# Gate/up loads moved onto the queue of the stores and fills, and a w_down half loaded sooner

## The chip, the cores and the metric

The kernel is one program on one NeuronCore of a Trainium2 chip. The metric is the device time of one launch in microseconds; lower is better. The kernel before took 619.9 us as the median of 8 runs (615.25 to 622.07 us). The profile is of one further execution, which took 621.76 us and whose span, from the core's first instruction to its last, is 620.0 us.

## The reference

The reference is the forward and the backward pass of a transformer block for one token (B = 1, S = 1, D = 1024), returned together. The parts that matter here, cut down:

```python
mod = silu(c) @ w_mod                      # six sections of 1024: sa, ca, ga, sb, cb, gb
h = layernorm(x) * (1 + ca) + sa
x = x + ga * attention(h)                  # 32 query heads, 4 kv heads, window of 4096 keys, Dh = 128
h = layernorm(x) * (1 + cb) + sb
g, u = h @ w_gate, h @ w_up                # 1024 x 3584 each
x = x + gb * ((sigmoid(g) * u) @ w_down)   # w_down is 3584 x 1024
# vjp with grad_out: gradients of x, k_cache, v_cache, wq, wo, w_gate, w_up, w_down, c, w_mod
```

All inputs and outputs are bf16. The gradients are large: those of `w_gate` and `w_up` are 7.3 MB each, that of `w_down` as much, and those of the two caches are 67 MB each. Only the last 4096 of 65,536 rows of a cache head take part, so most of the cache gradients is zero, and these zeros must be written too.

## The kernel before

The order of work is written out by hand, and each engine runs its own list in that order. All large buffers lie in one tile `arena`, whose places are reused again and again; whoever writes a place waits until its earlier readers and writers are done. Three queues issue transfers:

- SP's queue (hardware descriptors) issues most loads.
- POOL's queue (software descriptors) issues all large stores, a few loads, and the fills: `zero(n)` stores n megabytes (1 MiB each) of zeros into the cache gradients. There are 120 such pieces, and tables named `Z_...` say how many go where. Fills depend on nothing, so they keep the transfer engines supplied while the stores wait for compute.
- ACT's queue issues three tiny loads at the start.

Each queue issues in order. A transfer on POOL's queue also waits for the landing of the transfer issued eight places before it on that queue (eight semaphores go round), so at most eight POOL transfers are under way.

The parts in order: load the modulation weights, the keys, `wq` and the values; attention forward; two long matmul chains that make N (`n_ps`, L630) and B (`b_ps`, L683); the modulation sections; then the feed-forward stage, which is what the change touches; then the final stage, which computes and stores the other gradients.

Before the feed-forward stage, six tiles `B_t` (2 KiB per partition each) hold the product B. They are "parked": `park(p, ...)` transposes tile p into a PSUM bank, after which its place in the arena is free. Tiles 0 to 3 are parked early. Tiles 4 and 5 lie where the second half of a `w_down` block will lie, and are parked after the folds: `fold_tile` (L869) adds three modulation tiles on TensorE into two PSUM banks, which ScalarE copies out. The PSUM banks for this come from a rotation `rot`, at that point one bank of pool `psum` and two of pool `ppq`.

The feed-forward stage goes over 7 blocks q of 512 hidden columns. For each block:

- `load_ug` brings the block's columns of `w_up` and `w_gate` (2 MiB in all, rows of 1 KB) into one of two buffers; blocks q and q+2 share a buffer. `load_wd` brings the block's 512 rows of `w_down` in two halves of 512 KiB into one buffer.
- `front(q)` multiplies the loaded columns by h2 on TensorE, `gates` and `hh_ops` make the hidden values.
- For each half, `ffn_mm` uses `w_down` for the forward pass, `wd_ttr` (VectorE, L210, writing `junk`) for the backward pass, and `wd_outer` (VectorE, L206) overwrites the half by its gradient, which `store_wd` (L853, POOL) stores.
- `dug_part` makes the gradient of the gate/up activations as the row `dug_b`.
- In the loop over j, `ttr` (VectorE, L210) reads each of 8 slices of the gate/up buffer, `outer_act` (ScalarE, L241) overwrites it by its gradient, and `store_ug` (L867, POOL) stores slices 0-3, 4-5 and 6-7.

In the kernel before, `load_ug(q + 2, ...)` stands directly behind the store of the same slices and is issued by SP (L863), as is `load_wd` (L850). SP therefore waits, in turn, for the landing of each store and then issues the load into its place. Fills stand at three points of each iteration, `Z_FFN` gives the counts: after the store of slices 0-3, after the store of slices 6-7, and after the second `store_wd`. ScalarE also does `side()` jobs, transposes that later stages need, between these steps.

Of the kernel before, what the change touches and what calls it, by code (L numbers as in the profile page):

```python
# [10 lines left out]
P = 128  # L11
FP32 = mybir.dt.float32
BF16 = mybir.dt.bfloat16
# [6 lines left out]
D = 1024  # L20
# [27 lines left out]
Z_GA = 3  # L48
Z_CB = 2
Z_Q = [0] * 7 + [3]  # L50
# [4 lines left out]
Z_FOLD = (3, 4)  # L55
Z_FFN = [(1, 2, 2)] + [(1, 1, 2)] * 5 + [(2, 2, 2)]
Z_END = (3, 1, 1, 1, 1)

@with_exitstack
def kernel(  # L60
# [34 lines left out]
    px = ctx.enter_context(tc.tile_pool(name="px", bufs=1, space=bass.MemoryType.PSUM))  # L95
    ppq = ctx.enter_context(tc.tile_pool(name="ppq", bufs=2, space=bass.MemoryType.PSUM))

# [229 lines left out]
    B_off = [156, 158, 152, 154, 156, 158]  # L327
    B_t = [ar(o, 2) for o in B_off]

# [71 lines left out]

    rot[:] = [(psum, "mm"), (pna, "na"), (pgu, "gu"), (ppq, "pq"), (px, "x"), (pna, "na"), (ppq, "pq")]
    mod_ps = new_acc("mod_ps")
# [32 lines left out]

    jobs = []

    def side(n=1):
# [179 lines left out]
    for g in range(G):  # L619
        nbank = [(pna, ppq)[g % 2].tile([P, 512], FP32, name="n_ps", tag=("na", "pq")[g % 2]) for _ in range(2)]  # L620
        for t_ in range(KT):
# [50 lines left out]
    def bch(n=1):  # L672
        for _ in range(n):
            if not bq:
                return
            p, i, u = bq.pop(0)
            if i == 0:
                bbank[p] = [(pna, ppq)[p % 2].tile([P, 512], FP32, name="b_ps", tag=("na", "pq")[p % 2])
                            for _ in range(2)]
            for a in range(4):  # L680
                h = 4 * u + a
                for k in range(2):
                    mm = nc.tensor.matmul(bbank[p][k][:, :], lhsT=a4[:, p, h, :], rhs=wo_t[u][:, a, k * 512:(k + 1) * 512],  # L683
                                          start=(i == 0 and a == 0), stop=(i == 7 and a == 3))
            zero(Z_B[nbq - 1 - len(bq)], recent(mm, 3))
            if i == 7:
                for k in range(2):
                    o = B_t[p][:, k * 512:(k + 1) * 512]
                    if k == 0 or p == NBP - 1:
                        nc.scalar.copy(out=o, in_=bbank[p][k][:, :])  # L690
                    else:
                        cp(o, bbank[p][k][:, :])
# [132 lines left out]
    zero(Z_CB)  # L825
    rot[:] = [(psum, "mm"), (ppq, "pq"), (ppq, "pq")]

# [8 lines left out]
    jobs[:] = [tr_unit(v_nat[:, i // 4, (i % 4) * 1024:(i % 4 + 1) * 1024]) for i in range(16)]  # L836
    side(4)

# [21 lines left out]

    def load_ug(q, j0, n, eng=nc.sync):
        for k, view in ((0, wu_view), (1, wg_view)):
            eng.dma_start(out=ug_tile(q, k, j0, n), in_=ug_part(view, q, j0, n))  # L863

# [4 lines left out]
    def fold_tile(t):  # L869
# [11 lines left out]
        fold_ps.clear()  # L881

    fold_ps = []
    md_ps = new_acc("md_ps")
    for t in range(4):
        fold_tile(t)
    mod_tiles(md_ps, sb_t, range(4), True)
    load_ug(0, 0, 4, nc.gpsimd)
    load_ug(0, 4, 4, nc.gpsimd)
    load_wd(0, 0)  # L890
    zero(Z_FOLD[0])
# [8 lines left out]
    for t in range(4, 8):  # L900
        fold_tile(t)
    park(4, ppq, "pq")
    park(5, ppq, "pq")
    rot[:] = [(psum, "mm")]
    load_wd(0, 1)
    load_ug(1, 0, 4, nc.gpsimd)
    load_ug(1, 4, 4, nc.gpsimd)
    zero(Z_FOLD[1])
# [3 lines left out]
    dug_b2 = dug_b.rearrange("p (k f) -> p k f", k=2)  # L912
    junk = vt([P, D], "junk", BF16)
    dh2acc = vt([P, NB * KD], "dh2acc")
# [69 lines left out]
    for q in range(NB):  # L984
        z = Z_FFN[q]
        more = q + 1 < NB
        for j in range(KD):
            w = ug_v[:, q % 2, j // 4, j % 4, :, :].rearrange("p k f -> p (k f)")
            ttr(w, w, dug_b, dh2acc[:, q * KD + j:q * KD + j + 1])
            if j in (0, 2, 5) or (j == 6 and q < 4):  # L990
                side()
            outer_act(w, h2[:, j:j + 1], dug_b)
            if j == 0:
                if q == 0:
                    cp(ffn, ffn_ps)
# [39 lines left out]
    for p in range(NBP):  # L1035
        nc.scalar.copy(out=B_t[p], in_=BT_ps[p][:, :])
    rot[:] = [(psum, "mm"), (pna, "na"), (pgu, "gu"), (ppq, "pq"), (px, "x"), (pna, "na"), (ppq, "pq")]
    dh2 = vt([P, KD], "dh2")
# [269 lines left out]
```

## Time and profile before

| what | value |
|---|---|
| median of 8 runs | 619.9 us (615.25 to 622.07) |
| profiled execution, its time / its span | 621.76 us / 620.0 us |
| moved over HBM | 61.87 MB read, 185.60 MB written, 399 GB/s over the span |
| busy: PE, DVE, ACT, POOL | 391.9, 324.3, 282.1, 153.8 us |
| first stores of gate/up gradients, blocks 0 to 6, issued at | 319.06, 342.00, 376.50, 398.41, 420.87, 456.33, 477.16 us |

How to read it: an engine's busy time is no bound by itself. The page's row GB/s gives what the 16 transfer engines moved in each of 40 slices of 15.5 us. A long run of slices above 420 is a stretch in which transfers set the pace, and a slice well below it means that the transfer engines had nothing queued for part of it, or small pieces. The chain that ended last leads from the last instruction back to what released each step. A wait is listed as who waited, for whom, us in total, times, and the longest. The trace also has the time at which each transfer landed.

### The profile page before, as it was taken

What the parts mean: (1) busy time and instruction counts of PE and PEld (TensorE: products, weight loads), DVE (VectorE), ACT (ScalarE), POOL (GpSimd) and SP (SyncE); (2) the same over time, 40 slices, a digit from 0 to 9 for tenths busy, and PEclk for the clock granted to TensorE, in tenths of its full rate; (3) what the DMA queues carried; (4) which work ended last, traced back from release to release, by engine and by line L of the source; (5) the groups of instructions that cost most, each with busy time, mean ns of one, the idle gap of its engine ahead of it and who ended that gap; (6) DMA issues with size and microseconds to landing.
All of it is one profiled execution on the core that took longest, in us unless ns stands there. A gap on an engine that the chain in (4) does not pass through costs nothing.

```text
span 620.0 us, 10941 instructions
## 1 busy us (share of the span) xinstructions
PE 391.9 (63%) x4516; PEld 267.3 (43%) x4516; DVE 324.3 (52%) x616; ACT 282.1 (45%) x426; POOL 153.8 (25%) x249
## 2 busy tenths in 40 slices
PE   3996889999999989898244245341453466826200
PEld 3994434334345546558243234341342255826200
DVE  2745488999411020150468167772478279596500
ACT  3488414557211024246085438764287735834100
POOL 0002121222231212213223314323134442132220
PEclk9999598999999989998655555555555576555555
DMA  9999999999999999999999999999999999999995
GB/s 356 420 418 385 411 421 396 425 422 421 418 426 425 425 428 415 350 422 340 397 357 405 410 384 390 411 410 408 357 406 350 422 418 415 422 424 425 427 424 227
DMA packets 57105, 248.19 MB, mean 400 GB/s; under 512 B 5517, under 2 KB 15757, under 8 KB 36624
## 3 DMA queue, kind: packets, MB, share of 16 engines
q0 software_dynamic: 34656, 200.29, 84.1%
q1 hardware_dynamic: 22352, 47.20, 22.0%
q8 instruction: 35, 0.57, 0.4%
q14 instruction: 14, 0.11, 0.0%
q10 hardware_dynamic: 48, 0.01, 0.0%
HBM read 61.87 MB, written 185.60 MB: 399 GB/s over the span
## 4 chain that ended last, share of the span: by engine, by line
PE 39%; DMA 28%; DVE 12%; ACT 10%; issue 7%; POOL 1%; ACTq 0%; POOLq 0%; SPq 0%; DVEq 0%
PE b_ps L683 14%; DMA out_dram<-arena 14%; DMA arena<-in_B_w_down_dram 10%; PE n_ps L630 6%; ACT arena L241 4%; DVE junk L210 3%; DVE arena L193 3%; DMA out_dram<-zeros 3%; PE t_ps L592 2%; PE fold_ps L876 2%; ACT arena L833 2%; PE tp_wq L448 2%; DVE arena L210 1%; PE w_ps L393 1%; PE tp_side L832 1%
## 5 line engine op out<-in xcount | busy, mean ns | idle before, releaser
L169 POOL DMA_DIRECT2D out_dram<-zeros x114 | 62.9, 554 | 201.7 <-PE n_ps L630 54.9
L683 PE MATMUL b_ps<-arena 128*128 128x512 bf16 x384 | 89.7, 390 | 0.0
L832 PE MATMUL tp_side<-ident_bf,arena 128*128 128x128 bf16 x416 | 49.8, 297 | 53.4 <-ACT arena L833 44.8
L193 DVE TENSOR_TENSOR arena<-arena 128x2048 bf16<-128x2048 bf16 x64 | 76.6, 1223 | 3.4 <-PE n_ps L630 1.5
L630 PE MATMUL n_ps<-arena 128*128 128x512 bf16 x256 | 67.1, 386 | 6.1 <-DVE arena L193 4.5
L210 DVE CUSTOM_DVE_ANT_0 arena<-arena,scr 128x1024 bf16<-128x1024 bf16 x56 | 65.2, 1221 | 9.5 <-ACT scr L965 9.5
L833 ACT COPY arena<-tp_side 128x1024 bf16<-128x1024 bf16 x52 | 52.1, 1010 | 35.0 <-PE tp_side L832 34.8
L832 PEld LDWEIGHTS <-arena 128*128 128x128 bf16 x416 | 41.4, 137 | 58.9 <-issue 58.6
L241 ACT ACTIVATE arena<-scr,h 128x1024 bf16<-128x1024 bf16 x56 | 61.0, 1145 | 0.0
L683 PEld LDWEIGHTS <-arena 128*128 128x128 bf16 x384 | 37.7, 100 | 46.5 <-issue 7.3
L867 POOL DMA_DIRECT2D out_dram<-arena x42 | 30.8, 736 | 60.7 <-ACT arena L241 56.5
L630 PEld LDWEIGHTS <-arena 128*128 128x128 bf16 x256 | 25.1, 99 | 42.5 <-issue 18.0
L210 DVE CUSTOM_DVE_ANT_0 junk<-arena,b1k 128x1024 bf16<-128x1024 bf16 x28 | 34.2, 1223 | 13.7 <-DMA arena<-in_B_w_down_dram 13.2
L1129 ACT ACTIVATE arena<-ps_kv 128x512 bf16<-128x512 f32 x48 | 26.0, 687 | 32.3 <-PE ps_kv L1125 32.2
L1125 PE MATMUL ps_kv<-junk,arena 8*128 8x128 bf16 x256 | 27.2, 305 | 14.1 <-DVE arena L206 13.1
L594 ACT CAST arena<-t_ps 128x512 bf16<-128x512 f32 x56 | 30.1, 589 | 12.2 <-PE t_ps L592 12.2
L1125 PEld LDWEIGHTS <-arena 8*128 8x128 bf16 x256 | 25.3, 141 | 15.7 <-issue 15.7
L928 PE MATMUL fg<-h_bf,arena 128*128 128x1 bf16 x448 | 14.2, 166 | 25.9 <-DMA arena<-in_B_w_up_dram 18.9
L202 DVE CAST arena<-b_ps 128x512 bf16<-128x512 f32 x5 | 3.5, 692 | 47.1 <-PE b_ps L683 47.1
L853 POOL DMA_DIRECT2D out_dram<-arena x14 | 10.0, 717 | 63.9 <-DVE arena L206 57.2
L450 ACT COPY arena<-tp_wq 128x1024 bf16<-128x1024 bf16 x23 | 21.7, 1041 | 8.3 <-PE tp_wq L448 8.3
L928 PEld LDWEIGHTS <-arena 128*128 128x128 bf16 x448 | 13.6, 104 | 26.8 <-DMA arena<-in_B_w_up_dram 19.5
(294 smaller groups left out, 618.5 us busy)
## 6 DMA issues: line engine op xcount, KB each, us to landing
out_dram<-zeros POOLq DMA_DIRECT2D x114, 1024.0 KB, 11.3
out_dram<-arena POOLq DMA_DIRECT2D x32, 1024.0 KB, 19.4
out_dram<-arena POOLq DMA_DIRECT2D x36, 512.0 KB, 8.8
arena<-in_A_wq_dram SPq DMA_DIRECT2D x8, 1024.0 KB, 20.3
arena<-in_B_w_down_dram SPq DMA_DIRECT2D x14, 512.0 KB, 10.4
out_dram<-arena POOLq DMA_DIRECT2D x28, 256.0 KB, 8.4
arena<-in_A_wo_dram SPq DMA_DIRECT2D x6, 1024.0 KB, 6.7
arena<-in_w_mod_dram POOLq DMA_DIRECT2D x6, 1024.0 KB, 9.4
```

The source lines that it names most:

```text
L169: ins = nc.gpsimd.dma_start(out=region.bitcast(FP32), in_=zeros[:, :])
L193: return nc.vector.tensor_tensor(out=out, in0=a, in1=b, op=op)
L210: return nc.vector.tensor_tensor_reduce(out=out, in0=w, in1=b, scale=1.0, scalar=0.0, op0=ALU.mult, op1=ALU.add, accum_out=acc)
L241: return nc.scalar.activation(out=out, in_=b, func=ACT.Copy, scale=col)
L594: nc.scalar.copy(out=o, in_=ps)
L630: mm = nc.tensor.matmul(nbank[k][:, :], lhsT=k_nat[:, g, t_ * DH:(t_ + 1) * DH], rhs=vp[:, t_ % 2, 4 * k:4 * k + 4, :].rearrange("p h d -> ...
L683: mm = nc.tensor.matmul(bbank[p][k][:, :], lhsT=a4[:, p, h, :], rhs=wo_t[u][:, a, k * 512:(k + 1) * 512], start=(i == 0 and a == 0), stop= ...
L832: nc.tensor.transpose(tp[:, i * P:(i + 1) * P], blk[:, i * P:(i + 1) * P], ident_bf[:, :])
L833: nc.scalar.copy(out=blk, in_=tp[:, :])
L867: nc.gpsimd.dma_start(out=ug_part(view, q, j0, n), in_=ug_tile(q, k, j0, n))
L928: nc.tensor.matmul(gu[:, col + i:col + i + 1], lhsT=ug_v[:, q % 2, j // 4, j % 4, k, i * P:(i + 1) * P], rhs=h2_bf[:, j:j + 1], start=(j = ...
L1125: nc.tensor.matmul(ps[:, t4 * DH:(t4 + 1) * DH], lhsT=rows[32 * g:32 * g + HG, t_ * P:(t_ + 1) * P], rhs=hd[32 * g:32 * g + HG, :], start= ...
```

## The change

1. **Gate/up loads.** `load_ug` is issued by POOL for every block. In the loop it no longer stands behind the stores in the j loop. The load of slices 0-3 of block q+2 comes after the first `wd_ttr` of block q+1, that of slices 4-5 after the first `store_wd` and a fill, that of slices 6-7 after the second `store_wd`, ahead of a fill. SP's queue keeps only `w_down` loads in this stage.
2. **Fills.** `Z_FFN` has four points per iteration, one fill at each (31 fills before, 29 after, one fewer in the first block and one fewer in the last); `Z_CB`, ahead of the folds, goes from 2 to 3. One fill more is left over for the very end, where what is left is issued.
3. **B tiles.** Tile 5 lies in `junk` rather than in the arena; tile 4 is parked after the first of four `side` jobs, ahead of the folds. Both halves of `load_wd(0, ...)` then stand ahead of the folds.
4. **PSUM.** Pool `ppq` (two banks) becomes `ppq` and `prq` (one each), since tile 4 now occupies one of them from early on. The rotation for the folds has two banks rather than three.

```diff
-Z_CB = 2
+Z_CB = 3
-Z_FFN = [(1, 2, 2)] + [(1, 1, 2)] * 5 + [(2, 2, 2)]
+Z_FFN = [(1, 1, 1, 1)] * 6 + [(1, 2, 1, 1)]
...
-    ppq = ctx.enter_context(tc.tile_pool(name="ppq", bufs=2, space=bass.MemoryType.PSUM))
+    ppq = ctx.enter_context(tc.tile_pool(name="ppq", bufs=1, space=bass.MemoryType.PSUM))
+    prq = ctx.enter_context(tc.tile_pool(name="prq", bufs=1, space=bass.MemoryType.PSUM))
...
-    B_t = [ar(o, 2) for o in B_off]
+    junk = vt([P, D], "junk", BF16)
+    B_t = [ar(o, 2) for o in B_off[:5]] + [junk]
...
+    def bank_pair(name, odd):
+        pair = ((ppq, "pq"), (prq, "rq")) if odd % 2 else ((pna, "na"), (pna, "na"))
+        return [pl.tile([P, 512], FP32, name=name, tag=tag) for pl, tag in pair]
...
-    rot[:] = [(psum, "mm"), (ppq, "pq"), (ppq, "pq")]
+    rot[:] = [(psum, "mm"), (prq, "rq")]
...
-    side(4)
+    side(1)
+    park(4, ppq, "pq")
+    side(3)
...
-    def load_ug(q, j0, n, eng=nc.sync):
+    def load_ug(q, j0, n):
         for k, view in ((0, wu_view), (1, wg_view)):
-            eng.dma_start(out=ug_tile(q, k, j0, n), in_=ug_part(view, q, j0, n))
+            nc.gpsimd.dma_start(out=ug_tile(q, k, j0, n), in_=ug_part(view, q, j0, n))
...
+    load_wd(0, 0)
+    load_wd(0, 1)
     fold_ps = []
...
-    load_wd(0, 0)
     zero(Z_FOLD[0])
...
-    park(4, ppq, "pq")
-    park(5, ppq, "pq")
+    park(5, prq, "rq")
     rot[:] = [(psum, "mm")]
-    load_wd(0, 1)
...
             if j == 3:
                 store_ug(q, 0, 4)
                 zero(z[0])
-                if q + 2 < NB:
-                    load_ug(q + 2, 0, 4)
             if j == 5:
                 store_ug(q, 4, 2)
-                if q + 2 < NB:
-                    load_ug(q + 2, 4, 2)
         store_ug(q, 6, 2)
         zero(z[1])
         if more:
-            if q + 2 < NB:
-                load_ug(q + 2, 6, 2)
             front(q + 1)
             gates(q + 1)
             side()
             hh_ops(q + 1)
             ffn_mm(q + 1, 0)
             wd_ttr(q + 1, 0)
+            if q + 2 < NB:
+                load_ug(q + 2, 0, 4)
             wd_outer(q + 1, 0)
+            zero(z[2])
+            if q + 2 < NB:
+                load_ug(q + 2, 4, 2)
             side()
             ffn_mm(q + 1, 1)
             wd_ttr(q + 1, 1)
             side()
             dug_part(q + 1)
             wd_outer(q + 1, 1)
-            zero(z[2])
+            if q + 2 < NB:
+                load_ug(q + 2, 6, 2)
+            zero(z[3])
             if q + 2 < NB:
                 load_wd(q + 2, 0)
                 load_wd(q + 2, 1)
         else:
-            zero(z[2])
+            zero(z[2] + z[3])
```

The two places that allocated PSUM pairs for `n_ps` and `b_ps` call `bank_pair`, which gives the same banks under the new pool names.

More of the change, by code (lines that the diff above doesn't have):

```diff
@@ L400, in w01_fold @@
                 cp(o, v)
-    rot[:] = [(psum, "mm"), (pna, "na"), (pgu, "gu"), (ppq, "pq"), (px, "x"), (pna, "na"), (ppq, "pq")]
+    rot[:] = [(psum, "mm"), (pna, "na"), (pgu, "gu"), (ppq, "pq"), (px, "x"), (pna, "na"), (prq, "rq")]
     mod_ps = new_acc("mod_ps")
@@ L619 @@
     for g in range(G):
-        nbank = [(pna, ppq)[g % 2].tile([P, 512], FP32, name="n_ps", tag=("na", "pq")[g % 2]) for _ in range(2)]
+        nbank = bank_pair("n_ps", g)
         for t_ in range(KT):
@@ L677, in bch @@
             if i == 0:
-                bbank[p] = [(pna, ppq)[p % 2].tile([P, 512], FP32, name="b_ps", tag=("na", "pq")[p % 2])
-                            for _ in range(2)]
+                bbank[p] = bank_pair("b_ps", p)
             for a in range(4):
@@ L887 @@
     mod_tiles(md_ps, sb_t, range(4), True)
-    load_ug(0, 0, 4, nc.gpsimd)
-    load_ug(0, 4, 4, nc.gpsimd)
-    load_wd(0, 0)
+    load_ug(0, 0, 4)
+    load_ug(0, 4, 4)
     zero(Z_FOLD[0])
@@ L901 @@
         fold_tile(t)
-    park(4, ppq, "pq")
-    park(5, ppq, "pq")
+    park(5, prq, "rq")
     rot[:] = [(psum, "mm")]
-    load_wd(0, 1)
-    load_ug(1, 0, 4, nc.gpsimd)
-    load_ug(1, 4, 4, nc.gpsimd)
+    load_ug(1, 0, 4)
+    load_ug(1, 4, 4)
     zero(Z_FOLD[1])
@@ L912 @@
     dug_b2 = dug_b.rearrange("p (k f) -> p k f", k=2)
-    junk = vt([P, D], "junk", BF16)
     dh2acc = vt([P, NB * KD], "dh2acc")
@@ L1036 @@
         nc.scalar.copy(out=B_t[p], in_=BT_ps[p][:, :])
-    rot[:] = [(psum, "mm"), (pna, "na"), (pgu, "gu"), (ppq, "pq"), (px, "x"), (pna, "na"), (ppq, "pq")]
+    rot[:] = [(psum, "mm"), (pna, "na"), (pgu, "gu"), (ppq, "pq"), (px, "x"), (pna, "na"), (prq, "rq")]
     dh2 = vt([P, KD], "dh2")
```

## Prediction

> **What bounds the kernel now.** I read the page's throughput row first, then the waits, the chain, and last the windows and the issue times of one queue.
>
> ```profile
> GB/s 356 420 418 385 411 421 396 425 422 421 418 426 425 425 428 415 350 422 340 397 357 405 410 384 390 411 410 408 357 406 350 422 418 415 422 424 425 427 424 227
> ...
> q0 software_dynamic: 34656, 200.29, 84.1%
> q1 hardware_dynamic: 22352, 47.20, 22.0%
> ```
>
> Each number is 15.5 us. Most of the run moves 415 to 428 GB/s: the transfer engines set the pace. The weak part is slices 17 to 31 (248 to 480 us), the folds and the feed-forward stage. The sum below is therefore one of transfer time: the bytes stay the same, so time is won only where engines stood empty or moved slowly, and lost where new holes open. That part is 84% POOL's queue (q0) and else SP's (q1).
>
> ```profile
> SPq L863 <- DMA out_dram<-arena: 67.6, 24, 9.0
> ...
> SPq L850 <- DMA out_dram<-arena: 60.4, 12, 23.6
> ...
> POOL out_dram L853 <- DVE arena L206: 57.2, 11, 16.4
> POOL out_dram L867 <- ACT arena L241: 56.5, 17, 7.5
> ```
>
> SP waits for each store to land before a load may take its place, and POOL waits for compute (a `w_down` gradient from VectorE, a gate/up gradient from ScalarE). In POOL's waits the engines live on what is queued.
>
> ```profile
> 294.83 11.83 DMA arena<-in_B_w_down_dram
> ...
> 343.72 20.39 DMA arena<-in_B_w_down_dram
> ...
> 418.74 21.99 DMA arena<-in_B_w_down_dram
> ```
>
> In the chain (start, us, what), `w_down` loads take 20 and 22 us where the clean ones take 7.3 to 10.4 by their landings: SP issued them right behind six gate/up loads.
>
> ```profile
> 319.06 1.50 POOL L867 DMA_DIRECT2D out_dram<-arena  x2 [7.51 <-ACT arena L241]
> ...
> 342.00 1.52 POOL L867 DMA_DIRECT2D out_dram<-arena  x2 [6.68 <-ACT arena L241]
> ...
> 376.50 1.52 POOL L867 DMA_DIRECT2D out_dram<-arena  x2 [6.70 <-ACT arena L241]
> ...
> 456.33 1.52 POOL L867 DMA_DIRECT2D out_dram<-arena  x2 [6.67 <-ACT arena L241]
> ...
> 477.16 1.52 POOL L867 DMA_DIRECT2D out_dram<-arena  x2 [5.92 <-ACT arena L241]
> ```
>
> These are first stores of blocks 0, 1, 2, 5 and 6. The last step, 20.8 us, is compute alone: no loads are left. Blocks 0 to 5 take 137.3 us, 27.45 each, with steps of 34.5 and 35.5 where `front` or `wd_ttr` waited for a late load. A block moves 10.49 MB (gate/up 2.10 in and out, `w_down` 1.05 in and out, four fills 4.19), which is 24.7 us at 425 GB/s. So compute has room, and transfers and late loads share the blame.
>
> ```profile
> 284.00:286.00 2.00, 0.24 (x10) 0.24 (x10) 0.00 (x0) 0.71 (x1) 2.00 (x3) 1.00 0.63 162
> 302.00:304.00 2.00, 0.00 (x0) 0.00 (x0) 0.00 (x0) 0.00 (x0) 0.72 (x1) 0.50 1.04 362
> 318.00:320.00 2.00, 0.00 (x0) 0.00 (x0) 2.00 (x5) 2.00 (x3) 0.94 (x2) 0.50 0.43 169
> 448.00:450.00 2.00, 1.01 (x8) 0.85 (x8) 1.11 (x1) 0.90 (x2) 1.66 (x3) 0.50 0.56 209
> 464.00:466.00 2.00, 1.01 (x8) 0.74 (x7) 2.00 (x6) 0.90 (x2) 0.71 (x1) 0.50 1.05 410
> ```
>
> The last two columns are the engines' busy share and GB/s. At 284, 318 and 448 us the engines run dry (share 0.4 to 0.6). At 302 us they are busy at 362 GB/s, with POOL's gate/up loads in rows of 1 KB. At 464 us POOL's stores and fills alone give 410.
>
> **The change, step by step.** Durations are of the profiled execution: 621.76 us, 1.76 outside its 620.0 us span. Its median sibling is 619.9; I take the difference from the ledger and apply it to the median.
>
> **(a) Fold region.** Window 280:290 moves 305 GB/s, a hole of (425-305)*10/425 = 2.8 us. The added fill is 1.05 MB = 2.5 us, issued near 274.5 behind two others. The second `w_down` half, 0.52 MB = 1.2 us, was issued at 294.83 after tile 5's parking; now it needs only tile 4's, near 275. Together 3.7 us of supply for a hole of 2.8: -2.8. The first half was already issued at 253.11, so moving its line does nothing. Against it: the fill stands ahead of block 0's gate/up loads, which landed until 293.35, and `front(0)` began at 295.87, a slack of 2.5 us. So the bound is 0 to -2.8; I take -2.8, since the hole itself takes up the fill.
>
> **(b) Block 0.** VectorE waited for the late half until 306.69. Its work before ends near 302.4 (300.68 and two L206 of 0.88), so the second half starts 4.3 us earlier, the first store at 314.8 rather than 319.06. The fills ahead of it landed until 317.7; the hole in 318 to 322 (169 and 226 GB/s against 410, two us each: 1.2 + 0.9) closes: -2.1, bound 0 to -2.1. It does not shorten block 1 as much: its `w_down` loads wait for the first store's landing at 318.91, behind the same fills.
>
> **(c) Loads in one line.** In 320 to 449 us, 129 us at 395 GB/s, 51.0 MB go through. What is the rate in one line? By rows: block 1's four loads and one `w_down` half took 300.75 (landing of the fill ahead) to 307.9: 2.62 MB in 7.15 us, 367 GB/s. Gate/up loads 2.10/0.367 = 5.7 us, stores and fills 7.34/0.410 = 17.9, `w_down` loads 1.05/0.410 = 2.6: 26.2 us a block, 400 GB/s. Where the two queues ran together without holes (330 to 360 us) the windows show 404 to 413, say 407. I take the middle, 403: 51.0/0.403 = 126.5, -2.5 us. Ends: 400 gives -1.6, and 420 gives -7.7.
>
> A rule of the Trainium skill speaks against a gain in rate here: "DMA: Bandwidth & Descriptors", section "Issuing engines are not separate DMA queues", says that all issuers' transfers run on the same 16 engines and interleave, so the issuer saves only issue time. Reading the windows 190 to 230 us (POOL alone, 425) as what one line gives would make (c) -9.1 (51.0/0.425 = 119.9). But those are fills and no 1 KB loads; the 367 row is POOL's own. So I side with the rule: what (c) can win is the holes (366, 371, 382 and 321 GB/s in the 10-us windows from 320, 360, 380 and 440), not the mixing.
>
> **Waits that come with it.** POOL now issues 30 loads more in the loop, at 0.77 us (POOL's gate/up loads) 23 us, on 40 busy in 129: no bound. A load waits for the landing of the store it overwrites; that store stands eight places before it on the queue or near it, so the queue's own limit would have held it anyway. Behind a waiting load stand a `w_down` gradient store, for which SP's next load waits, and a fill. Relative to a block's first store t, and with the unstalled block (456.33, 465.18, 468.65): the `w_down` store is ready at t+8.9; the load before it is released when the first store pair, issued over 1.5 us, has landed. With landing time L, the load's own issue taking 1.5 us, the store goes at t+3+L, lands at t+3+2L, and SP's load lands Lw later; the next block's `wd_ttr` wants it at t+T+5.3. So T >= 2L + Lw - 2.3. With L = 8.6 and Lw = 8.7 (near the middle of the L867 and clean L850 landings) that is 23.6: under 26.2. The gate/up loads in last place follow the second `w_down` store, t+12.3, are out by t+13.8 and land by t+13.8+L, wanted at t+T+5: T >= 17.4.
>
> The second rule that speaks against: "SBUF — State Buffer", section "SBUF: two separate sides", says that VectorE in a two-port mode locks POOL out, so that POOL's queue cannot write descriptors while SP's is immune. By it, each of six loads a block could lose one L206 of 0.88 us, 5.3 us a block, 26 in five. The row: L867, the same shape, issued beside a VectorE that is busy over half of the time, has a mean of 736 ns against 770 for loads issued beside an idle one. I take the row: 0. If the rule held, the 9 us of queued transfers (L) would cover most of it.
>
> **(d) Small ones.** Two PSUM banks for the folds: TensorE takes about 0.87 us per bank (6.96 us for eight), ScalarE's copy 0.59, so the bank is free again while the other fills: 0, at most 0.2 us for eight tiles, 1.6. Parking tile 4 moves 0.61 us of TensorE. The fills taken from blocks 0 and 6 are in the bytes of (a) and of the end, where slices run at 422 to 427: 2.5 us of work moved, neither won nor lost. In blocks 5 and 6 nothing is left to load in either kernel, and the hole at 476 us (window 470:480, 323 GB/s) stays. For new small holes I charge +0.8, two rows like that at 446 us (306 against 410: 0.5 us each) less what the fill before the second half covers.
>
> Sum: -2.8 - 2.1 - 2.5 + 0.8 = -6.6 us; 621.76 would be 615.2, and the median 619.9 becomes **613.3 us**.
>
> **Rivals.**
> 1. Slower, by the loop above: the load that waits for its store holds back the `w_down` store. With L = 11 and Lw = 10, T is 29.7; for five blocks 5*(29.7-27.45) = +11.3, less (a) and (b) where they remain (half of 4.9), and the fill: about +6, 626 us. It decides from T near 28.5, that is L above 10.6 at Lw = 9.6. For it: landings of L867 stores of 10 to 13 us at 342 to 349 us, and 24 waits of SP for just these landings, which now are POOL's. Against it: L falls when fewer transfers are queued, and after the waiting load a block has 5 MB queued, over 12 us.
> 2. Hidden anyway: the fill only stands ahead of the loads of block 0, the earlier `w_down` half only lets VectorE wait for the next one, and the rate in line is 398 (-1). With half of (b) that is about 618 us. For it: block 1's loads wait for the store that lands at 318.91.
> 3. More: in-line loads overlap with stores, 420 GB/s: -7.7 in place of -2.5, 608 us. For it: 425 of POOL alone; against it: 362 and 367 with loads.
>
> **Numbers.** A measurement of this kernel tells about 0.5% (3.1 us) from no change. Likeliest 0.42 (613.3, its own range 610 to 616), rival 1 0.20, rival 2 0.22, rival 3 0.16. Faster (under 616.8): the likeliest, rival 3 and a tenth of rival 2, 0.60; same 0.20; slower (over 623.0) 0.20. The range 606 to 625 leaves out the better part of rival 3's gain below and half of rival 1 above.
>
> **What would show it.** (a) Window 280:290 above 380 GB/s and SP's second `w_down` issue near 275. (b) First store near 315, no row under 300 at 318 to 322. (c) First stores 25 to 27 us apart with no step above 30, no wait of TensorE L928 for a gate/up load over 3 us, `w_down` landings under 12 us, 400 to 408 GB/s in the stage. (d) Fold matmuls in no more than 7.2 us. It is wrong if POOL's waits for store landings at the load line pass 4 us a block and VectorE still waits for `w_down` (rival 1), or if first stores come no sooner (rival 2).

## The result and the profile after

| | before | after |
|---|---|---|
| median, us | 619.02 (614.6 to 626.48, 32 runs) | 612.41 (611.86 to 614.42, 11 runs) |
| ratio, 95% interval | 1 | 0.9905 (0.9878 to 0.9933) |
| profiled execution / its span, us | 621.76 / 620.0 | 612.05 / 610.3 |

The change makes the kernel faster by 6.6 us by the medians and by 5.9 us by the ratio; the interval reaches from 4.1 to 7.6. The ratios leave out slow runs of before, those more than 1.5% above its fastest, one of 957 us timed beside e1 to e4 among them. The profiled pair differs by 9.7 us, 3.1 more than the medians; below it turns out that 1.1 to 2.2 us of this difference arose ahead of everything the loads and fills touch.

The lines of after have other numbers than those of before:

| what | before | after |
|---|---|---|
| gate/up stores (POOL) | L867 | L874 |
| `w_down` stores (POOL) | L853 | L860 |
| gate/up loads | L863 | L870 |
| `w_down` loads (SP) | L850 | L857 |
| products of `front` (TensorE) | L928 | L933 |
| products of `ffn_mm` (TensorE) | L945 | L950 |
| `wd_ttr` and `ttr`, `wd_outer` (VectorE) | L210, L206 | L211, L207 |
| `outer_act` (ScalarE) | L241 | L242 |

A "hole" below is a stretch in which the transfer engines moved clearly less than their neighbouring stretches; "the line" is POOL's queue once it carries gate/up loads, stores and fills together.

First the throughput row and the two queues of the page of after. A slice is 15.3 us here.

```profile
GB/s 353 419 417 389 404 425 411 418 420 420 422 424 425 427 425 422 395 423 401 398 420 410 387 402 414 406 410 411 409 417 344 424 415 415 422 427 425 424 425 221
...
q0 software_dynamic: 37696, 210.78, 89.9%
q1 hardware_dynamic: 11632, 36.71, 17.3%
```

The weak slices of before (350, 340, 357 and 357, between 248 and 450 us) have become 395, 401, 420 and 409. One slice stays at 344: it is 458 to 473 us, which holds the end of the feed-forward stage, where nothing is left to load. The bytes are the same; 10.5 MB of them have moved from SP's queue to POOL's.

Then windows of 10 us, and the four microseconds from 318 us. After the stretch and its length, the columns are busy time of TensorE, its weight loads, VectorE, ScalarE and POOL with the number of instructions, the granted clock, the transfer engines' busy share, and GB/s. First two windows of before:

```profile
280.00:290.00 10.00, 7.59 (x144) 7.53 (x142) 0.60 (x4) 4.97 (x8) 4.66 (x7) 0.83 0.92 305
...
470.00:480.00 10.00, 3.79 (x31) 3.13 (x30) 9.70 (x22) 9.22 (x10) 3.87 (x6) 0.50 0.89 327
```

And of after:

```profile
280.00:290.00 10.00, 8.80 (x163) 8.43 (x163) 0.58 (x4) 6.07 (x9) 4.66 (x7) 0.83 1.17 397
310.00:320.00 10.00, 3.93 (x84) 3.50 (x81) 3.94 (x11) 8.48 (x11) 5.44 (x8) 0.50 1.09 415
318.00:322.00 4.00, 0.00 (x0) 0.00 (x0) 0.09 (x1) 0.53 (x1) 3.04 (x5) 0.50 1.11 420
330.00:340.00 10.00, 4.53 (x48) 3.78 (x49) 7.30 (x16) 4.76 (x5) 5.35 (x8) 0.50 1.05 388
450.00:460.00 10.00, 2.70 (x36) 2.27 (x36) 5.53 (x13) 3.04 (x3) 3.26 (x5) 0.50 1.10 416
460.00:470.00 10.00, 3.85 (x32) 3.20 (x31) 9.78 (x22) 9.15 (x10) 2.10 (x4) 0.50 0.87 320
```

The hole at 280 us (305 GB/s) and the one at 318 (169 and 226) are gone. At 330 there is a new small one, (425-388)*10/425 = 0.9 us. At 460 the old one of 470 to 480 us (327) stands at its new place.

POOL's first stores of the seven blocks in after (start, us, line, and in brackets how long POOL waited and for whom):

```profile
311.67 1.50 POOL L874 DMA_DIRECT2D out_dram<-arena  x2 [6.94 <-ACT arena L242]
...
343.64 1.51 POOL L874 DMA_DIRECT2D out_dram<-arena  x2 [5.81 <-ACT arena L242]
...
365.76 1.51 POOL L874 DMA_DIRECT2D out_dram<-arena  x2 [4.50 <-ACT arena L242]
...
390.47 1.50 POOL L874 DMA_DIRECT2D out_dram<-arena  x2 [3.57 <-ACT arena L242]
...
416.48 1.50 POOL L874 DMA_DIRECT2D out_dram<-arena  x2 [3.90 <-ACT arena L242]
...
441.81 1.50 POOL L874 DMA_DIRECT2D out_dram<-arena  x2 [3.73 <-ACT arena L242]
...
467.23 1.51 POOL L874 DMA_DIRECT2D out_dram<-arena  x2 [7.17 <-ACT arena L242]
```

The steps are 32.0, 22.1, 24.7, 26.0, 25.3 and 25.4 us. From block 0 to block 5 it is 130.1 us, 26.03 a block. The first step is long, the second short, the others even.

Last the waits of after in 265 to 500 us (engine, line, who ended the wait: us in all, times, longest):

```profile
POOL out_dram L874 <- ACT arena L242: 43.1, 14, 7.2
PEld L950 <- DMA arena<-in_B_w_down_dram: 39.5, 10, 9.7
...
DVE junk L211 <- DMA arena<-in_B_w_down_dram: 25.0, 9, 8.3
...
POOL out_dram L860 <- DVE arena L207: 17.9, 7, 7.7
...
PEld L933 <- DMA arena<-in_B_w_up_dram: 8.0, 4, 2.9
...
POOL arena L870 <- DMA out_dram<-zeros: 4.3, 4, 2.3
POOL arena L870 <- DMA out_dram<-arena: 3.7, 5, 1.3
```

The wait for stores and fills that the change gave to POOL is in the last two rows: 8.0 us in five blocks, 1.6 a block. (Two smaller rows of L870, not shown, are 2.8 us for the landing of earlier gate/up loads and 2.0 us for TensorE.) POOL's wait for `w_down` gradients, 57.2 us before, is 17.9. VectorE and TensorE still wait for `w_down` loads. VectorE's longest wait, 8.3 us, is for block 1's; e8 and e11 below tell what it costs.

**Where the time came from.** Both kernels move nearly the same bytes in nearly the same order, so I add up the bytes in the two traces and compare the moment at which each has moved as many. This is the ledger used from here on. The last two columns set after against two other profiles without the change, which come up again at the end: e10 is before once more, e12 is before with its PSUM pool split as in after.

| MB moved | at, before (us) | after minus before (us) | step | after minus e10 | after minus e12 |
|---|---|---|---|---|---|
| 100 | 243 | -0.5 | | -0.3 | 0.1 |
| 112 | | -2.2 | -1.7, near 104 to 106 MB | -1.1 | 0.1 |
| 122 | 301 | -4.6 | -2.4, the fold region | -3.5 | -2.0 |
| 132 | | -6.9 | -2.3, block 0 | -7.1 | -4.2 |
| 180 | 449 | -9.7 | -2.8, blocks 1 to 5 | -10.6 | -8.4 |
| 247 | | -9.8 | -0.1, the end | -10.7 | -8.5 |

Each row stands on single profiles. The step of the fold region is 2.4, 2.4 and 2.1 us in the three columns, that of block 0 2.3, 3.6 and 2.2, that of blocks 1 to 5 2.8, 3.5 and 4.2, so a step is known to about a microsecond and no better.

### The profile page after: what moved, and what is told of

Its sections match the earlier page's. It is cut to its first block, busy times and chain, and to the rows that moved or that the text cites. A ratio compares the mean times of both kernels' runs of the same rounds, so it can differ in the third digit from the quotient of the medians.

```text
span 610.3 us, 10920 instructions
## 1 busy us (share of the span) xinstructions
PE 389.9 (64%) x4516; PEld 266.2 (44%) x4516; DVE 325.5 (53%) x616; ACT 282.4 (46%) x426; POOL 176.0 (29%) x279
## 4 chain that ended last, share of the span: by engine, by line
PE 35%; DMA 30%; DVE 15%; ACT 8%; issue 8%; POOL 1%; ACTq 0%; POOLq 0%; DVEq 0%; SPq 0%
PE b_ps L688 14%; DMA out_dram<-arena 12%; DMA arena<-in_B_w_down_dram 10%; PE n_ps L636 6%; DMA out_dram<-zeros 6%; DVE arena L194 4%; DVE arena L211 3%; DVE arena L207 3%; DVE junk L211 3%; ACT arena L242 2%; PE t_ps L598 2%; DMA arena<-in_B_w_gate_dram 2%; PE tp_wq L454 2%; PE w_ps L395 1%; PE tp_k L435 1%
## 5 line engine op out<-in xcount | busy, mean ns | idle before, releaser
L211 DVE CUSTOM_DVE_ANT_0 arena<-arena,scr 128x1024 bf16<-128x1024 bf16 x56 | 65.2, 1221 | 9.1 <-ACT scr L970 9.1
L636 PE MATMUL n_ps<-arena 128*128 128x512 bf16 x256 | 65.7, 378 | 6.4 <-DVE arena L194 4.7
L837 PEld LDWEIGHTS <-arena 128*128 128x128 bf16 x416 | 41.1, 137 | 56.3 <-issue 56.1
L242 ACT ACTIVATE arena<-scr,h 128x1024 bf16<-128x1024 bf16 x56 | 61.0, 1145 | 0.0
L688 PEld LDWEIGHTS <-arena 128*128 128x128 bf16 x384 | 37.8, 101 | 46.4 <-issue 7.1
L211 DVE CUSTOM_DVE_ANT_0 junk<-arena,b1k 128x1024 bf16<-128x1024 bf16 x28 | 34.2, 1223 | 25.5 <-DMA arena<-in_B_w_down_dram 25.0
L874 POOL DMA_DIRECT2D out_dram<-arena x42 | 30.7, 733 | 50.9 <-ACT arena L242 43.1
L636 PEld LDWEIGHTS <-arena 128*128 128x128 bf16 x256 | 24.6, 97 | 41.7 <-issue 16.3
L1135 ACT ACTIVATE arena<-ps_kv 128x512 bf16<-128x512 f32 x48 | 26.2, 687 | 29.5 <-PE ps_kv L1131 29.3
L950 PE MATMUL fg<-hh_bf,arena 128*128 128x1 bf16 x224 | 8.0, 166 | 38.7 <-DMA arena<-in_B_w_down_dram 34.7
L1131 PEld LDWEIGHTS <-arena 8*128 8x128 bf16 x256 | 25.3, 141 | 16.0 <-issue 15.9
L950 PEld LDWEIGHTS <-arena 128*128 128x128 bf16 x224 | 7.1, 104 | 41.6 <-DMA arena<-in_B_w_down_dram 39.5
L207 DVE TENSOR_SCALAR arena<-arena,cs_col 128x4096 bf16<-128x4096 bf16 (+1 forms) x16 | 16.1, 1020 | 11.2 <-DMA out_dram<-arena 10.9
## 6 DMA issues: line engine op xcount, KB each, us to landing
arena<-in_B_w_down_dram SPq DMA_DIRECT2D x14, 512.0 KB, 10.6
```

The costliest lines, as they stand in the source:

```text
L207: return nc.vector.tensor_scalar(out=out, in0=a, scalar1=s1, scalar2=None, op0=op0)
L211: return nc.vector.tensor_tensor_reduce(out=out, in0=w, in1=b, scale=1.0, scalar=0.0, op0=ALU.mult, op1=ALU.add, accum_out=acc)
L242: return nc.scalar.activation(out=out, in_=b, func=ACT.Copy, scale=col)
L636: mm = nc.tensor.matmul(nbank[k][:, :], lhsT=k_nat[:, g, t_ * DH:(t_ + 1) * DH], rhs=vp[:, t_ % 2, 4 * k:4 * k + 4, :].rearrange("p h d -> ...
L837: nc.tensor.transpose(tp[:, i * P:(i + 1) * P], blk[:, i * P:(i + 1) * P], ident_bf[:, :])
L874: nc.gpsimd.dma_start(out=ug_part(view, q, j0, n), in_=ug_tile(q, k, j0, n))
```

## The experiments

Three theories went to the chip. The ledger theory is the prediction's: transfer time is won hole by hole, in the sizes (a) to (c). The line theory says that the gain is that of having loads, stores and fills on one queue. The waiting-load theory is rival 1: a load on POOL that waits for a store holds back all that is behind it. Unless an experiment says otherwise, a diff is against after, and "to after" is the difference of the medians. The experiments were timed in three groups, each beside its own runs of before (medians 619.05, 619.62 and 619.81; after's own 619.02), so where a microsecond matters the ratios are set against each other too; a ratio's interval is 1.6 to 2.7 us to each side. All of them do the whole computation; the fills only change their places.

**e1, the loads alone.** Before, with the loop of after (loads on POOL in their new places); the fold region as before.

```diff
--- before
+++ e1
-Z_FFN = [(1, 2, 2)] + [(1, 1, 2)] * 5 + [(2, 2, 2)]
+Z_FFN = [(1, 1, 2, 1)] + [(1, 1, 1, 1)] * 5 + [(1, 2, 2, 1)]
...
-    def load_ug(q, j0, n, eng=nc.sync):
+    def load_ug(q, j0, n, eng=nc.gpsimd):
```

> The kernel before with the gate/up loads alone moved: POOL issues them, at the new places, with the fills of the stage split over four points but as many as before (31). Nothing is changed ahead of the feed-forward stage. Ledger theory (the change wins by closing holes, and the largest two lie in the folds and in block 0): only term (c) is left, 1.7 to 2.5 us, so about 617 where before is 619.0. Line theory (nearly all of the gain comes from the loads in one line with the stores): 5 us or more, 614 or less. Waiting-load theory (a load on POOL holds back the w_down store): 622 or more.

Measured: 616.22 us, ratio 0.995 (0.9925 to 0.9976), 2.8 us less than before. The windows of the fold region and of block 0 keep their holes:

```profile
280.00:290.00 10.00, 7.67 (x149) 7.61 (x147) 0.66 (x4) 5.08 (x9) 4.68 (x7) 0.83 0.93 295
...
318.00:322.00 4.00, 0.99 (x9) 0.83 (x9) 4.00 (x7) 4.00 (x5) 1.75 (x3) 0.50 0.44 144
```

**e2, the fold region alone.** After, with the gate/up loads of the loop back on SP in their old places.

```diff
-Z_FFN = [(1, 1, 1, 1)] * 6 + [(1, 2, 1, 1)]
+Z_FFN = [(1, 1, 2)] * 6 + [(1, 2, 2)]
...
-    def load_ug(q, j0, n):
+    def load_ug(q, j0, n, eng=nc.sync):
...
                 zero(z[0])
+                if q + 2 < NB:
+                    load_ug(q + 2, 0, 4)
```

> The changed kernel with the gate/up loads of blocks 2 to 6 put back on SP, behind their stores, with three fill points and 29 fills in the stage as after. Tile 5 in junk, tile 4 parked early, the w_down half early, the third fill ahead of the folds and the two-bank rotation stay. Ledger theory: terms (a) and (b), 2.8 + 2.1, so about 614 where before is 619.0, with the hole at 280 to 290 us closed and the first store of block 0 some 4 us earlier. Line theory: less than 2 us, 617 or more, since late gate/up loads still stop blocks 2 and 5.

Measured: 614.30 us, 0.9936 (0.9907 to 0.9966), 4.75 us less than before. Window 280 to 290 us moves 398 GB/s, the first store of block 0 goes at 310.73. A `w_down` load again takes 21.0 us, as in before. The two parts add up to -7.55 against -6.6 together, which their intervals allow. In the ledger e2 runs with after up to 132 MB (-6.7 us to before) and falls behind it by 1.5 us up to 180 MB (-8.1). Both results stand where the ledger theory put them; the line theory wanted 614 or less from e1, the waiting-load theory 622 or more.

**e3, new places, but SP's queue.** The loads stay where after has them in the program; those of blocks 2 to 6 are issued by SP.

```diff
-            nc.gpsimd.dma_start(out=ug_tile(q, k, j0, n), in_=ug_part(view, q, j0, n))
+            (nc.sync if q > 1 else nc.gpsimd).dma_start(out=ug_tile(q, k, j0, n), in_=ug_part(view, q, j0, n))
```

> The changed kernel with the loads of blocks 2 to 6 issued by SP, all else as after, their places in the order too. If the place decides: as the changed kernel, 612 to 613. If the line decides (a load on SP's queue [...]is late, and w_down loads wait behind it): (c) is lost, 615 to 617, with w_down loads of 15 us and more to landing again.

Measured: 618.12 us, 0.9981 (0.9947 to 1.0015), +5.7 to after. This is a miss of the ledger theory: (c), 2.5 us by its sum, can't hold a loss of 5.7. The ledger of e3 stays near that of after up to 185 MB and then falls from -9.8 to -1.8. Two windows show the place:

```profile
460.00:470.00 10.00, 4.89 (x65) 4.17 (x62) 8.54 (x18) 5.08 (x6) 3.32 (x5) 0.50 0.58 216
470.00:480.00 10.00, 3.04 (x24) 2.55 (x24) 7.89 (x19) 10.00 (x10) 3.49 (x5) 0.50 0.61 218
```

After moves 320 and 407 GB/s there. The waits of 438 to 480 us show who waited there:

```profile
POOL out_dram L860 <- DVE arena L207: 18.4, 2, 16.9
...
PEld L933 <- DMA arena<-in_B_w_up_dram: 16.6, 3, 6.9
```

One of the last block's gate/up loads and its second `w_down` load, issued by SP, landed 22.2 and 18.9 us after issue while POOL's stores and fills ran ahead beside them (no gate/up load of after took over 12.6 us). When POOL had nothing left to send but a gradient that was not computed, the engines stood nearly half empty. In after, what stands behind a load in POOL's queue goes behind it; here the stores and fills did not wait for SP's loads. Whether the sharing of the transfer engines or SP's own order (a `w_down` load behind waiting gate/up loads) did more was not tried. One profile shows this, and the twelve times of e3 scatter from 612.8 to 622.1, so it may not happen in each execution.

Nor is the queue the whole of it. By their traces e2 and e3 send the loads from SP in the same order; in the loop they differ only in one fill of each block, which stands behind the first `w_down` store in e3 and behind the second in e2. Yet e3 is 3.8 us slower by the medians and 2.8 by the ratios, whose intervals overlap. So loads on SP's queue cost 1.9 us with one order of the fills (e2) and 5.7 with another (e3), and how much of the 5.7 is the fill's is open.

**e4, old places, but POOL's queue.** The loads are issued by POOL where before has them: right behind the store whose buffer they take.

```diff
                 zero(z[0])
+                if q + 2 < NB:
+                    load_ug(q + 2, 0, 4)
             if j == 5:
                 store_ug(q, 4, 2)
+                if q + 2 < NB:
+                    load_ug(q + 2, 4, 2)
...
             wd_ttr(q + 1, 0)
-            if q + 2 < NB:
-                load_ug(q + 2, 0, 4)
```

> The changed kernel with the loads on POOL but directly behind the stores whose places they take, as they stood before. POOL then waits at each load for the landing of the store just issued, with the next stores and fills behind it. Waiting-load theory (the place is what makes one line possible): three waits of 4 to 9 us per block, first stores 30 us apart and more, 625 to 660. If such waits are covered by what is queued: 612 to 616.

Measured: 634.97 us, 1.026 (1.0226 to 1.0294), +22.6 to after. Its waits of 300 to 500 us, and a window:

```profile
POOL arena L870 <- DMA out_dram<-arena: 69.8, 15, 8.4
```

```profile
330.00:340.00 10.00, 4.07 (x32) 3.42 (x33) 8.69 (x18) 6.67 (x7) 7.24 (x11) 0.50 0.84 280
...
450.00:460.00 10.00, 4.21 (x38) 3.64 (x38) 8.78 (x20) 6.97 (x7) 6.65 (x10) 0.50 0.77 256
```

POOL waits 69.8 us at these loads for stores to land, instead of 3.7, in 15 waits of 4.7 us on average; the gate/up stores take 6.6 us (median) to land. Meanwhile it issues nothing and the engines run short, once a block (256 to 287 GB/s in five windows). The waiting-load theory is right here: the one line pays only with the places that the change gives it.

**e5, one fill less ahead of the folds.**

```diff
-Z_CB = 3
+Z_CB = 2
```

> The changed kernel (612.4) with two fills ahead of the folds instead of three; the third goes to the very end. Ledger theory: the hole of 2.8 us at 280 to 290 us has only the w_down half (1.2 us) to fill it, so 1.6 us is lost: 614.0. If the fill merely stands ahead of block 0's loads, nothing is lost: 612.4 or a little less.

Measured: 615.71 us, 0.9965 (0.994 to 0.9991), +3.3 to after (3.7 by the ratios); 1.6 was expected.

```profile
280.00:290.00 10.00, 9.88 (x199) 9.15 (x197) 0.88 (x4) 7.68 (x13) 5.35 (x8) 1.00 1.00 309
```

The hole of before (305) is back at 309, though the second `w_down` half was loaded early as in after. The half's packets had moved by about 284 us, ahead of the hole, and gave nothing to it: the fill is what closes this hole.

**e6 and e9, the second `w_down` half late.** e6 moves only the load's place in the program:

```diff
 load_wd(0, 0)
-load_wd(0, 1)
...
+    load_wd(0, 1)
     load_ug(1, 0, 4)
```

> The changed kernel with only the second w_down half of block 0 issued where it was before, after the folds; tile 4 is parked early all the same. Ledger theory: block 0's first store is some 4 us later again, the hole at its front reopens (2.1 us), and the fold hole keeps its fill: 614.5. If the late half is covered by the four fills queued behind block 1's loads: 612.4.

Measured: 613.16 us, 0.9905 (0.9876 to 0.9933), no difference that these runs tell, and for a plain reason: SP issued the load at 271.77 us as in after (272.10). SP has nothing else to issue in between, so the load goes as soon as tile 4 is parked, wherever it stands in the program. The experiment tested nothing. e9 does it by the parking, as before has it:

```diff
-    side(1)
-    park(4, ppq, "pq")
-    side(3)
+    side(4)
...
+    park(4, ppq, "pq")
     park(5, prq, "rq")
     rot[:] = [(psum, "mm")]
+    load_wd(0, 1)
```

> The changed kernel with tile 4 parked after the folds, as before, so that the second w_down half of block 0 really is issued late (near 292 us; moving the line alone had left its issue at 272). Third fill, loads on POOL and the two-bank rotation stay. Ledger theory: the fold hole keeps its fill, block 0's first store is some 4 us later and the hole at its front (318 to 322 us) reopens: 2 us, 614.5. If the early half is worth nothing: 612.4.

Measured: 614.01 us, 0.9904 (0.9866 to 0.9941): +1.6 to after by the medians, nothing by the ratios. The load went at 291.04 us, the first store at 317.69 instead of 311.67. The fold region stays filled, which shows once more that the third fill does it alone, and the hole of block 0 is back in part:

```profile
280.00:290.00 10.00, 8.81 (x186) 8.38 (x184) 0.58 (x4) 6.78 (x11) 4.84 (x8) 1.00 1.09 393
310.00:320.00 10.00, 3.65 (x31) 3.15 (x31) 9.33 (x17) 8.90 (x10) 2.23 (x4) 0.50 0.93 343
318.00:322.00 4.00, 2.61 (x73) 2.61 (x73) 1.58 (x4) 3.95 (x5) 3.07 (x5) 0.50 0.81 221
```

The ledger loses 2.7 us to after between 128 and 132 MB and regains 1.1 by 150. So the trace shows the mechanism, and the times leave its worth between 0 and about 2 us.

**e7, fills into the last hole.** The hole at 460 us stands while POOL waits for block 6's gradients. e7 takes two of the fills that wait for the end and puts them behind the stores of the block before.

```diff
-Z_FFN = [(1, 1, 1, 1)] * 6 + [(1, 2, 1, 1)]
-Z_END = (3, 1, 1, 1, 1)
+Z_FFN = [(1, 1, 1, 1)] * 5 + [(1, 1, 2, 2)] + [(1, 2, 1, 1)]
+Z_END = (1, 1, 1, 1, 1)
```

> The changed kernel with two fills taken from the three after the feed-forward stage and put behind the w_down stores of block 5 (Z_FFN of block 5 is 1, 1, 2, 2; the first of Z_END is 1). In the changed kernel the window 460 to 470 us moves 320 GB/s where its neighbours move 416: a hole of 2.3 us, with no loads left. Ledger theory: the fills close it, 610.3. If compute sets the pace from here to the end: 612.4. If the fills are missed where they were taken from: 613 or more, with a hole near 485 us.

Measured: 609.16 us, 0.985 (0.981 to 0.989), -3.2 to after. Window 460 to 470 us now moves 424 GB/s instead of 320, worth (424-320)*10/424 = 2.5 us:

```profile
460.00:470.00 10.00, 3.13 (x25) 2.55 (x24) 8.77 (x16) 8.71 (x9) 3.15 (x5) 0.50 1.12 424
```

**e8, fewer fills ahead of block 1.** Two fills go from ahead of the loop to behind block 0, so that block 1 gets its loads sooner.

```diff
-Z_FOLD = (3, 4)
-Z_FFN = [(1, 1, 1, 1)] * 6 + [(1, 2, 1, 1)]
+Z_FOLD = (3, 2)
+Z_FFN = [(1, 1, 2, 2)] + [(1, 1, 1, 1)] * 5 + [(1, 2, 1, 1)]
```

> The changed kernel with two of the four fills that stand ahead of block 0's w_down stores moved behind them (second of Z_FOLD 2 instead of 4, Z_FFN of block 0 is 1, 1, 2, 2). In the changed kernel block 0 to block 1 takes 32.0 us, since the w_down stores of block 0 land behind these fills and block 1's w_down loads wait for them. First stores of block 0 and 1 then stand some 27 us apart. Ledger theory (late compute costs only what the transfer engines lose by it; the windows 330 to 360 us are at 388 to 397 instead of 411): 1 us or less, 611.4 to 612.4. If the late block is on the path itself: 4 to 5 us, 608.

Measured: 614.31 us, 0.9915 (0.9885 to 0.9945), +1.9 to after (0.6 by the ratios) where 0 to -1 was expected. The step from block 0 to block 1 fell from 32.0 to 26.6 us as expected (310.96 to 337.56), and it won nothing. A new hole opened ahead of it:

```profile
310.00:320.00 10.00, 3.57 (x80) 3.30 (x79) 3.24 (x9) 7.77 (x10) 6.38 (x10) 0.50 0.99 345
```

That hole is worth (425-345)*10/425 = 1.9 us. The two fills had been the work that kept the engines busy up to there. Since e8 moves the block and opens a hole at once, it does not tell by itself that a late block is free; e11 is the cleaner test.

**e11, both lessons.** e7, and one more fill moved from ahead of the loop into the hole at 330 us.

```diff
-Z_FOLD = (3, 4)
-Z_FFN = [(1, 1, 1, 1)] * 6 + [(1, 2, 1, 1)]
-Z_END = (3, 1, 1, 1, 1)
+Z_FOLD = (3, 3)
+Z_FFN = [(1, 1, 2, 1)] + [(1, 1, 1, 1)] * 4 + [(1, 1, 2, 2)] + [(1, 2, 1, 1)]
+Z_END = (1, 1, 1, 1, 1)
```

> The kernel with two fills moved to block 5 (609.2), and one of the four fills ahead of block 0's w_down stores moved behind them (second of Z_FOLD 3, Z_FFN of block 0 is 1, 1, 2, 1). Moving two had opened a hole of 1.7 us at 310 to 320 and closed one of 1.3 at 330 to 360. Ledger theory: one leaves the first closed and closes most of the second (330 to 340 moves 344 there): 608.0 to 609. If three fills are too few as cover: 610.

Measured: 608.78 us, 0.9828 (0.9785 to 0.9871): faster than after (whose interval begins at 0.9878) and than before. Both holes of after are closed:

```profile
330.00:340.00 10.00, 3.87 (x32) 3.21 (x31) 8.89 (x16) 7.98 (x8) 3.52 (x6) 0.50 1.09 415
...
460.00:470.00 10.00, 3.88 (x32) 3.39 (x32) 9.87 (x21) 8.91 (x9) 2.85 (x5) 0.50 1.13 424
```

Against e7 it gains 0.4 us by the medians and 1.4 by the ratios, which these runs don't tell from nothing. Yet block 1's first store goes at 339.41 us, where e7 has it at 345.11, and no hole opens ahead of it (409 GB/s in 310 to 320 us). So the 5.7 us by which block 1 comes later in e7 cost 0.4 to 1.4 us, no more than the hole that stands beside it there (344 GB/s in 330 to 340 us, (425-344)*10/425 = 1.9 us): late compute cost what the transfer engines lost by it.

**e10 and e12, the clock at 95 us.** The ledger's second row, 1.7 us near 105 MB, falls where no load or fill has changed. e10 is before once more, in one profile; e12 is before with the pool of two PSUM banks split in two, and the places that use the banks renamed.

```diff
--- before
+++ e12
-    ppq = ctx.enter_context(tc.tile_pool(name="ppq", bufs=2, space=bass.MemoryType.PSUM))
+    ppq = ctx.enter_context(tc.tile_pool(name="ppq", bufs=1, space=bass.MemoryType.PSUM))
+    prq = ctx.enter_context(tc.tile_pool(name="prq", bufs=1, space=bass.MemoryType.PSUM))
```

> The kernel before, unchanged, once more. In the profile of before the chain N on TensorE began 2.2 us later than in the changed kernel, at 70 to 100 us, long before anything that the change touches, with a granted clock of 0.53 instead of 0.79 in 70 to 75 us. If that is chance, this profile may show 97 to 98 us as the changed kernel does for the copy that stands at 99.7 in the first; if it belongs to the program, 99.7 again.

> The kernel before with its pool of two PSUM banks written as two pools of one each, in all places, and nothing else changed. If the 2.2 us at 70 to 100 us come from how banks are laid out, they show here: the copy at 99.7 us in before stands at 97.5. If not, at 99.7. The time otherwise is that of before, 615 to 622.

Measured, one time each: e10 622.62 us, e12 620.42 us; both lie in the scatter of before. What they show of the clock is told in the last section.

## Why the prediction was right, and where its reasons were not

**The sum** was -6.6 us, from 619.9 to 613.3; the medians differ by 6.6 (5.9 by the ratio), and after's is 612.41. In part that is luck, since two terms held for other reasons than given. A few rates that I gave for windows of before are off by 1 to 5 GB/s (the trace has 367, 372, 387 and 320 from 320, 360, 380 and 440 us, and 327 in 470 to 480); no sum rests on them.

**(a) Fold region, -2.8 predicted.** The size held: the ledger gives -2.4, and taking the fill away costs 3.3 us. The step that failed is "together 3.7 us of supply for a hole of 2.8". The fill alone filled it (e5, e9). SP issued the half at 272.10, near the 275 I wrote, and just for that reason it had landed ahead of the hole. That the fill might make block 0's loads late, my bound towards 0, didn't come about: block 0's first store went at 311.67 instead of 319.06.

**(b) Block 0, -2.1 predicted.** -2.3 in the ledger; undoing it (e9) reopens the hole and costs 1.6 us by the medians, though nothing by the ratios. The first store came 3.1 us sooner than the 314.8 that I had worked out, but most of that is not the half's: e12, which changes only the PSUM pool, has it at 316.48 instead of 319.06. The step "it does not shorten block 1 as much" was too mild: block 1's first store, 342.00 before, is at 343.64, and the step of 32.0 us breaks my own "no step above 30", as does a `w_down` landing of 12.9 us the "under 12". e11 shows why it mattered little: the line was full most of that while.

**(c) Loads in one line, -2.5 predicted.** -2.8 in the ledger of blocks 1 to 5, where my +0.8 for small holes is to be set off too (net -1.7 predicted), and -2.8 by e1 alone. But e2, with the loads on SP as before, has won 1.3 of the ledger's 2.8 too, and taking the loads back costs 1.9 by its median: 1.9 is the better figure for the loads beside the other parts. 26.2 us a block were predicted, 26.03 measured. In the steady line of after, the spacing of landings is 1.36 us for a gate/up load of 0.52 MB (385 GB/s), 1.3 for a gate/up store of that size, 1.29 for a `w_down` store of it and 2.45 for a fill of 1.05 MB. With my 2.6 for the `w_down` loads, a block's bytes come to four such loads, four such stores, two `w_down` stores and four fills: 5.4 + 5.2 + 2.6 + 9.8 + 2.6 = 25.6 us. The terms for loads (5.7) and for the rest (17.9) were each a little high.

The prediction sided with the Trainium skill's rule that issuers share the same 16 engines ("DMA: Bandwidth & Descriptors", section "Issuing engines are not separate DMA queues") and drew from it that (c) can win holes and nothing by the mixing. As to rate this case agrees: after moves 387 to 420 GB/s in the slices of the loop, not the 425 of fills alone. What the sum missed is that the queue decides more than the rate: it decides who is late. e3 moves the same bytes and loses 5.7 us; in its profile loads on SP's queue land up to 22.2 us after issue and the end of the stage is nearly half empty (with the fills in their old places, e2, the loss is 1.9). I had the evidence, the `w_down` landings of 20 and 22 us in before, and used it only for the holes inside the blocks.

**Waits that come with it.** Costed at nothing, and 8.0 us in all came, behind queued transfers. Rival 1 was no phantom: e4 shows it at +22.6 us, and the places decide. The formula for it, T >= 2L + Lw - 2.3, named the wrong loop: with after's median landings (L 9.2, Lw 10.6) it asks for 26.7 us, and the last four steps average 25.4. The chain of waits of after runs through another: a `w_down` load of 11.71 us from 392.38, then VectorE from 404.11 until the next load can go at 418.21, 25.8 us. That is nearly the line's own 25.6, so the two are near balance, and no run tells which of them leads in these blocks. The line was full there: 410 GB/s from 350 to 458 us.

```profile
392.38 11.71 DMA arena<-in_B_w_down_dram
404.11 1.22 DVE junk L211
...
416.07 1.14 DVE arena L211
418.21 11.22 DMA arena<-in_B_w_down_dram
```

The Trainium skill's other rule against the change ("SBUF — State Buffer", section "SBUF: two separate sides") would have cost 26 us in five blocks by my estimate, and nothing of it shows: a gate/up load of the loop (L870) issues in 731 ns, an L874 store in 733, as before (736). Whether VectorE ran in such a mode at all, no trace here tells.

**(d)** Two banks for the folds cost little: the matmuls of four tiles took 6.3 and 7.2 us, where before has 6.0 and 7.1, and the copies out of the banks waited 3.6 us in nine waits. The charge of +0.8 for new holes is about what the windows show (0.9 at 330 to 340 us).

**The medians, taken apart.** Undone one at a time from after, the fill is worth 3.3 us (e5), the early half 1.6 (e9), the loads 1.9 (e2): 6.8, against 6.6 for all; by the ratios 3.7, 0 and 1.9, or 5.6 against 5.9. Either way the sum leaves nothing for the split of the PSUM pool, but each term has an interval of about two microseconds, so it doesn't rule a share of it out.

## What to carry to other kernels

When the transfer engines are the bound, count their holes in bytes, and put stores that depend on nothing into those where no load is left; moving two fills (e7) won half of what the whole change did. Here loads could share an in-order queue with stores when each stood where the store it waits for had nearly landed (1.6 us a block), not right behind it (22.6 us more in all). Compute that came 5.7 us late cost 1.4 us at most, since the queue had work for most of that time (e11). Loads on a second queue beside a full one came late, up to 22.2 us after issue, which cost 1.9 to 5.7 us in all, the more when nothing was left to send.

## What the runs showed of the hardware that was not expected

TensorE's instructions up to the folds are the same in both kernels but for the pool that their PSUM banks come from. Yet its granted clock differs at 95 to 100 us (the seventh column, after the five busy times). First before and its second profile e10, then after, then e12, which differs from before in the split pool alone:

```profile
95.00:100.00 5.00, 4.96 (x15) 1.89 (x15) 3.77 (x4) 0.27 (x1) 0.53 (x1) 0.66 0.99 361
```

```profile
95.00:100.00 5.00, 5.00 (x14) 1.64 (x13) 3.22 (x4) 0.00 (x0) 0.53 (x1) 0.50 1.09 392
```

```profile
95.00:100.00 5.00, 4.82 (x22) 2.12 (x22) 4.86 (x5) 2.16 (x4) 0.87 (x2) 1.00 1.10 403
```

```profile
95.00:100.00 5.00, 4.82 (x24) 2.11 (x22) 4.86 (x5) 2.45 (x5) 1.06 (x2) 1.00 1.16 410
```

The three profiles with one pool of two banks (before, e1, e10) have the dip: 0.50 to 0.70. The eleven with the split pool have a clock of 1.00 there. The work behind it runs later with the dip: a modulation load that waits for TensorE is issued by POOL at 250.65 to 251.81 us in the three and at 247.40 to 249.79 in the eleven. The ledger's step near 105 MB follows it: it is 1.7 us against before, 0.8 against e10 and none against e12. So the split accounts for 1.1 to 2.2 us of the profiled pair's difference, the rest being the scatter of single profiles. Why splitting the pool should move the clock is not settled, nor is its worth in the median: one run each of e10 and e12 doesn't tell 2 us.
